# Scores and transposed keys from one series of products, in a gated linear attention with a feed-forward net

## The chip, the cores and the metric

The kernel runs on one core of a Trainium2 chip. The metric is the device time of one execution in microseconds. Three runs of the kernel before gave 528.78 to 529.15 us, median 529.03 us. Its profiled execution took 527.96 us, with a span of 526.4 us from the first to the last instruction.

## The reference

Two parts follow each other. The first is a gated linear attention over 4 batches of 8 heads, 768 tokens and 48 channels a head, with a 48 x 48 state for each head; the second is a feed-forward net on the 3072 x 384 result, with 2048 hidden channels and an exact gelu.

```python
for t in range(S):
    state = alpha[:, :, t, :, None] * state + np.einsum('bhd,bhe->bhde', k[:, :, t], v[:, :, t])
    y[:, :, t] = np.einsum('bhd,bhde->bhe', q[:, :, t], state)
...
h = x @ w_in
g = 0.5 * h * (1.0 + erf(h * inv_sqrt2))
return (g @ w_out).astype(np.float32)
```

## The kernel before

**Units.** The tokens are worked in 12 groups g of 256 (three groups make a batch) and two halves u of four heads: 24 units, numbered n = 2g + u. Names carry both, as s_6_0 for g = 6, u = 0. For each unit, alpha, keys and queries lie in one tile `akq0` or `akq1` (by g), with channels on partitions: two heads of 48 channels in the two halves of 64 partitions, two such pairs, and 256 tokens in four chunks of 64.

**The steps of a unit.** VectorE scans alpha forward (L256) and multiplies the queries by the running products, in place (L261; from the fourth group on GpSimd does this). It scans backward (L265) and multiplies the keys (L268). TensorE then forms the scores of each chunk (`scores`, L284: 16 products with 64 columns of keys as weights and 64 columns of queries moving, each in a quadrant of the array) and transposes the keys (`turned`, L293: four 128 x 128 transposes), both into one two-bank PSUM tile `s`. ScalarE copies the transposed keys out (`turned_out`, tile kn, L300), VectorE masks the scores (`masked`, tile ss, L305). TensorE's step `inside` takes 16 products of masked scores with values (L326) and 16, or 12 in the last group of a batch, of transposed keys with values (the keys' products, L344), into the PSUM tile `ybank`. VectorE adds the latter up to states (`chain`, L361 and L363), and TensorE's `outer` adds states times queries (L390). ScalarE and VectorE split the result into a high and a low part x (L438, L442; in the first groups with a product by -1, the step minus, L447, that leaves the rest in PSUM), and small DMAs complete the tile.

**The net.** A step (g, f) takes 256 tokens and 256 of the 2048 hidden channels: gemm1 (L469, 18 products), the gelu twice on ScalarE (L481 rounded, L482 full), the low part as their difference (L487 on VectorE, or by L491 and L495), and gemm2 (L508, 12 products) into two accumulators. When the steps pass to another group, the accumulators are copied or added to a tile `part` (L525 on ScalarE, L523 and L527 on VectorE). The weights come as 64-bit floats in 16 pieces, a to p, converted by VectorE (L187, L193, L206, L215, L224, L234) and ScalarE (L183, L203) into a high and a low tile (wih and wil, woh and wol).

**The order of work.** All steps are objects with an engine, a cost from the table `COST`, dependencies and a rank; the string `ORDER` ranks the units (numbers) and the pieces (letters). A planner in the kernel simulates the engines with these costs, picks the ready step of least rank, and gives the engines their instructions in that order. `late` units yield to the net's steps; `RATE` and others model the DMAs. So a changed cost moves steps on all engines.

```python
ORDER = "0 1 a b 2 c 3 d 4 e 5 f g h i j k l m n o p"
...
d["scores"] = op("PE", "scores", lambda: (scores(g, u), turned(g, u)), [d["back"], d["q"], p.get("mask"), p.get("kn")], rank=r)
d["kn"] = op("ACT", "kn", lambda: turned_out(g, u), [d["scores"], p.get("inside")], rank=-1)
d["mask"] = op("DVE", "mask", lambda: masked(g, u), [d["scores"], p.get("inside")], rank=-1)
```

Of the kernel before, what the change touches and what calls it, by code (L numbers as in the profile page):

```python
# [8 lines left out]
F32 = mybir.dt.float32  # L9
# [6 lines left out]
ALU = mybir.AluOpType  # L16
# [24 lines left out]
def gla_then_gelu_ffn(ctx: ExitStack, tc: tile.TileContext, q, k, v, alpha, akq, w_in, w_out, out):  # L41
    nc = tc.nc
# [60 lines left out]
    for i in range(NB):  # L103
        vbuf.append(const.tile([P, 2, H * D + DR], F32, name=f"vn{i}"))
        data.append(const.tile([P, NU, 3, 2, G], F32, name=f"akq{i}"))

    for t in vbuf:
# [139 lines left out]
    def ahead(g, u):  # L247
# [3 lines left out]
        pe = work.tile([P, 2], F32, tag="pe", bufs=6, name=f"pe_{g}_{u}")  # L251
        cur[g, u] = dict(pe=pe, qt=qt, kt=kt)

# [18 lines left out]
    def ends_batch(g, j):  # L272
        return g % GPB == GPB - 1 and j == NCH - 1

    def scores(g, u):
        d = cur[g, u]
        d["s"] = ps_s.tile([P, 2, BANK], F32, tag="s", name=f"s_{g}_{u}")
        for i in range(2):
            for j in range(NCH):
                c, o = j // 2, slice((j % 2) * CS, (j % 2 + 1) * CS)  # L280
                t, e = slice(j * CS, (j + 1) * CS), (2 * i + c) * CS
# [6 lines left out]
    def turned(g, u):  # L288
        d = cur[g, u]
        for i in range(2):  # L290
            for c in range(2):
                e = (2 + c) * C
                nc.tensor.transpose(  # L293
                    out=d["s"][:, i, e : e + C], in_=d["kt"][:, i, c * C : (c + 1) * C], identity=ident
                )

    def turned_out(g, u):
        d = cur[g, u]
        d["kn"] = work.tile([P, 2, 2 * P], F32, tag="kn", bufs=1, name=f"kn_{g}_{u}")
        nc.scalar.copy(d["kn"], d["s"][:, :, 2 * C : 4 * C])  # L300

    def masked(g, u):
        d = cur[g, u]
        d["ss"] = work.tile([P, 2, NCH, CS], F32, tag="ss", bufs=1, name=f"ss_{g}_{u}")
        nc.vector.tensor_tensor(  # L305
            out=d["ss"],
            in0=d["s"][:, :, : 2 * C].rearrange("p h (c t) -> p h c t", t=CS),
            in1=mask.unsqueeze(1).unsqueeze(1).to_broadcast([P, 2, NCH, CS]),
            op=ALU.mult,
        )  # L310
# [4 lines left out]
    def inside(g, u):  # L315
        d = cur[g, u]
        vn = vbuf[g % NB]
        for i in range(2):
            for j in range(NCH):
                c, b = j // 2, j % 2  # L320
                r, t = slice(b * CS, (b + 1) * CS), (2 * i + c) * CS
                for h in range(2):
# [10 lines left out]
                    )  # L333
        for j in range(NCH):
            if ends_batch(g, j):
                continue
            c, b = j // 2, j % 2
            r = slice(b * CS, (b + 1) * CS)
            for i in range(2):
                t = 2 * C + (2 * i + c) * D  # L340
                for h in range(2):
                    o = slice(h * DP, (h + 1) * DP)
                    e = (4 * u + 2 * i + h) * D
                    nc.tensor.matmul(  # L344
                        ybank[o, b, t : t + D],
                        lhsT=d["kn"][r, i, c * P + h * DP : c * P + (h + 1) * DP],
                        rhs=vn[r, c, e : e + D],
                        start=False,
                        stop=True,
                        skip_group_check=True,  # L350
                    )

# [24 lines left out]
    def outside_part(g, u):  # L377
        d = cur[g, u]
        for c in range(NCH // 2):
            for i in range(2):  # L380
                for bb, h in ((0, 0), (0, 1), (1, 0), (1, 1)):
                    b = bb if g >= NSB else bb ^ h
                    j = 2 * c + b
                    if g % GPB == 0 and j == 0:
# [7 lines left out]
                        lhsT=states[u][j][r, i],  # L392
                        rhs=d["qt"][r, i, j * CS : (j + 1) * CS],
                        start=False,
# [261 lines left out]
    def plan_unit(n):  # L656
# [171 lines left out]

    bus, lanes, used_lanes = [0.0], [0.0] * LANES, [0]

# [142 lines left out]
```

## Time and profile before

| | |
|---|---|
| median of three runs | 529.03 us |
| profiled execution | 527.96 us |
| its span | 526.4 us |
| mean granted TensorE clock | 0.977 |
| TensorE (PE) busy | 504.8 us, 96% |
| VectorE (DVE) busy | 303.9 us, 58% |
| ScalarE (ACT) busy | 221.4 us, 42% |
| GpSimd (POOL) busy | 33.1 us, 6% |

The granted clock is a share of full speed: 1.00 is 2.4 GHz, 0.50 is 1.2 GHz. PEld is TensorE's weight load, which runs beside the products. A row of the time line gives the start, the duration, the engine, the line, what it writes and reads, how many instructions are drawn together, and in brackets how long the engine was idle before it and what it then waited for. A row of the chain gives start, duration and what ran, on the path that ended last; a product of 32-bit floats leaves two records, so 16 products are x32 there.

### The profile page before, as it was taken

Reading aid. Unit: us, or ns where it says so; the run is one execution under the profiler, and the core shown is the slowest. Engines: PE = TensorE matmul, PEld = TensorE weight load, DVE = VectorE, ACT = ScalarE, POOL = GpSimd, SP = SyncE. Lnnn points to the kernel's source line nnn. Section 1 sums busy time; section 2 is a strip of 40 time slices with the busy share of each in tenths; the row PEclk is TensorE's granted clock in tenths of the full one; section 3 lists DMA queues with packets and bytes.
Section 4 is the critical chain, followed back from the end, with each engine's and each line's share of the span. In section 5 each row is a group of like instructions: output and inputs, shape, how many; then the busy total and the mean of one; then the engine's idle time right before and its main releaser. Section 6 shows DMA issues by size and latency. Waiting matters only on the chain.

```text
span 526.4 us, 13851 instructions
## 1 busy us (share of the span) xinstructions
PE 504.8 (96%) x5994; PEld 487.1 (93%) x5994; DVE 303.9 (58%) x599; ACT 221.4 (42%) x462; POOL 33.1 (6%) x45
## 2 busy tenths in 40 slices
PE   6689899989999999999999999999999999999996
PEld 6578889989999999999999999999999999999995
DVE  6999999999948675866765677142242121211211
ACT  2466767545444454543545345343423222222221
POOL 1000010000001100100100010000000000000000
PEclk9559999999999999999999999999999999999999
DMA  8866472243012423422323322000000000000001
GB/s 307 322 197 212 136 227 88 94 121 121 1 60 79 152 76 92 129 80 68 121 77 97 128 65 78 1 32 17 1 32 16 1 30 1 32 0 1 31 1 34
DMA packets 15249, 44.20 MB, mean 84 GB/s; under 512 B 2224, under 2 KB 5728, under 8 KB 15184
## 3 DMA queue, kind: packets, MB, share of 16 engines
q1 hardware_dynamic: 13520, 38.44, 22.3%
q0 software_dynamic: 1232, 4.33, 2.3%
q8 instruction: 49, 0.80, 0.6%
q10 hardware_dynamic: 432, 0.49, 0.3%
q14 instruction: 16, 0.13, 0.1%
HBM read 36.18 MB, written 4.72 MB: 78 GB/s over the span
## 4 chain that ended last, share of the span: by engine, by line
PE 80%; DVE 13%; DMA 3%; issue 2%; ACT 1%; SPq 0%; DVEq 0%; ACTq 0%
PE hp L469 35%; PE acc L508 35%; PE ybank L390 2%; DVE rp L265 2%; PE ybank L326 2%; PE s L293 2%; PE s L284 2%; DVE pp L256 2%; PE ybank L344 2%; DMA st<-in_moe_w_in_dram 1%; DVE w L193 1%; DMA akq<-in_akq_dram 1%; DVE st L224 1%; DVE u L187 1%; DVE state L363 1%
## 5 line engine op out<-in xcount | busy, mean ns | idle before, releaser
L469 PE MATMUL hp<-x,wih 128*128 128x256 f32 x1152 | 213.7, 286 | 0.0
L469 PEld LDWEIGHTS hp<-x,wih 128*128 128x128 f32 x1152 | 183.2, 192 | 0.8
L469 PE MATMUL hp<-x,wil 128*128 128x256 f32 x576 | 163.5, 284 | 0.0
L481 ACT ACTIVATE ghi<-hp 128x512 fp32r<-128x512 f32 x96 | 57.5, 599 | 226.1 <-PE hp L469 224.2
L487 DVE TENSOR_TENSOR glo<-hp,ghi 128x512 fp32r<-128x512 f32 x86 | 59.3, 690 | 155.7 <-ACT hp L482 155.7
L508 PE MATMUL acc<-woh,ghi 128*128 128x384 f32 x384 | 131.8, 343 | 2.2 <-ACT part L525 1.5
L508 PE MATMUL acc<-wol,ghi 128*128 128x384 f32 x384 | 128.7, 335 | 0.0
L469 PEld LDWEIGHTS hp<-x,wil 128*128 128x128 f32 x576 | 110.7, 192 | 0.0
L508 PE MATMUL acc<-woh,glo 128*128 128x384 f32 x384 | 82.3, 335 | 0.4 <-DVE glo L487 0.4
L508 PEld LDWEIGHTS acc<-woh,ghi 128*128 128x128 f32 x384 | 72.3, 188 | 3.7 <-ACT part L525 1.7
L508 PEld LDWEIGHTS acc<-wol,ghi 128*128 128x128 f32 x384 | 72.5, 189 | 0.1
L508 PEld LDWEIGHTS acc<-woh,glo 128*128 128x128 f32 x384 | 67.9, 188 | 0.7 <-DVE glo L487 0.7
L482 ACT ACTIVATE hp<-hp 128x512 f32<-128x512 f32 x96 | 57.1, 594 | 0.0
L265 DVE TENSOR_TENSOR_SCAN rp<-akq,rp,top 128x255 f32<-128x255 f32 x48 | 39.0, 852 | 0.2
L261 POOL TENSOR_TENSOR akq<-akq,pp 128x512 f32<-128x512 f32 x18 | 23.3, 1293 | 232.9 <-DVE pe L257 183.8
L256 DVE TENSOR_TENSOR_SCAN pp<-akq,top 128x256 f32<-128x256 f32 x48 | 30.4, 675 | 9.4 <-DMA akq<-in_akq_dram 9.4
L390 PEld LDWEIGHTS ybank<-akq,state 48*48 48x48 f32 x704 | 15.6, 125 | 9.1 <-DVE state L363 5.1
L363 DVE TENSOR_TENSOR state<-ybank,state 128x96 f32<-128x96 f32 x80 | 20.5, 256 | 6.1 <-PE ybank L344 3.8
L442 DVE TENSOR_TENSOR x<-ybank,x 64x256 fp32r<-64x256 f32 (+3 forms) x54 | 19.2, 356 | 7.2 <-ACT x L438 6.3
L390 PE MATMUL ybank<-akq,state 48*48 48x64 f32 x704 | 19.3, 228 | 4.2 <-DVE state L363 4.2
L438 ACT CAST x<-ybank 64x256 fp32r<-64x256 f32 (+4 forms) x60 | 19.9, 332 | 7.1 <-PE ybank L390 6.4
L326 PEld LDWEIGHTS ybank<-ss,vn 64*64 64x64 f32 x768 | 14.2, 141 | 9.1 <-DVE ss L305 2.8
(67 smaller groups left out, 410.2 us busy)
## 6 DMA issues: line engine op xcount, KB each, us to landing
akq<-in_akq_dram SPq DMA_DIRECT2D x22, 768.0 KB, 4.8
st<-in_moe_w_in_dram SPq DMA_DIRECT2D x8, 768.0 KB, 4.5
st<-in_moe_w_out_dram SPq DMA_DIRECT2D x8, 768.0 KB, 4.5
vn<-in_v_dram SPq DMA_DIRECT2D x12, 384.0 KB, 3.6
out_dram<-part POOLq DMA_DIRECT2D x11, 384.0 KB, 3.4
x<-z SPq DMA_DIRECT2D x63, 32.0 KB, 2.0
akq<-in_akq_dram SPq DMA_DIRECT2D x2, 512.0 KB, 4.9
akq<-in_akq_dram SPq DMA_DIRECT2D x2, 256.0 KB, 3.4
```

What stands on the lines that cost most here:

```text
L256: nc.vector.tensor_tensor_scan(pp[:, i], at[:, i], top, MID, ALU.mult, ALU.min)
L261: (nc.vector if g < NSB else nc.gpsimd).tensor_tensor(out=qt, in0=qt, in1=pp, op=ALU.mult)
L265: nc.vector.tensor_tensor_scan(rp[:, i, G - 2 :: -1], at[:, i, G - 1 : 0 : -1], top[:, 1:], rp[:, i, G - 1 :], ALU.mult, ALU.min)
L326: nc.tensor.matmul(ybank[o, b, t : t + CS], lhsT=vn[r, c, e : e + DP], rhs=d["ss"][r, h, 2 * i + c, :], start=(i == 0 and c == 0), stop=(j ...
L363: d["chain"] = nc.vector.tensor_tensor(out=st[j + 1], in0=new, in1=st[j], op=ALU.add)
L390: ins = nc.tensor.matmul(ybank[o, b, t : t + CS], lhsT=states[u][j][r, i], rhs=d["qt"][r, i, j * CS : (j + 1) * CS], start=False, stop=Tru ...
L438: nc.scalar.copy(hi, y)
L469: nc.tensor.matmul(hp[:, j, :], lhsT=a[:, j, i * P : (i + 1) * P], rhs=x[:, i, :], start=(j == 0 and i == 0 and n == 0), stop=(i == NK - 1 ...
L481: nc.scalar.activation(ghi, hp, AF.Gelu)
L482: nc.scalar.activation(hp, hp, AF.Gelu)
L487: nc.vector.tensor_tensor(out=glo, in0=hp, in1=ghi.bitcast(F32), op=ALU.subtract)
L508: nc.tensor.matmul(acc[t], lhsT=a[:, j, t * C : (t + 1) * C], rhs=w[:, j, :], start=(first and j == 0 and k == 0 and w is wo_hi[f]), stop= ...
```

## The change

A tile qk0 or qk1 (by u) holds the queries times the running products, and behind each chunk's 64 columns 48 columns of an identity matrix, written once at the start by GpSimd. The scores' 16 products move these 112 columns, so that each gives a chunk's scores and its transposed keys; the four transposes are gone. ScalarE's copy is 384 columns wide, into one fixed tile. The keys' products run in another order, in which the two row halves b alternate. The multiplication of the queries writes to qk, for which it waits for outer of the unit before the last; the load of the next keys no longer waits for outer. The planner has lower costs for scores, kn and inside, a lower DMA rate with a later beginning, and another `ORDER`. GpSimd's DMA ring is smaller.

```diff
@@ planner's table
-RATE, ALONE, LATENCY, SMALL = 400e3, 290e3, 2.1, 50e3
+RATE, ALONE, LATENCY, SMALL, BEGIN = 350e3, 290e3, 2.1, 50e3, 2.2
-    scan=1.62, back=2.05, q=1.35, qv=0.62, scores=1.2, kn=0.6, mask=0.62, inside=1.2, chain=1.15, outer=0.85, carry=0.26,
+    scan=1.62, back=2.05, q=1.35, qv=0.62, scores=1.0, kn=0.5, mask=0.62, inside=1.05, chain=1.15, outer=0.85, carry=0.26,
-ORDER = "0 1 a b 2 c 3 d 4 e 5 f g h i j k l m n o p"
+ORDER = "0 a 1 2 b c 3 d 4 e 5 6 f 7 g h i j k l m n o p"
@@ constants
+    KW = CS + D
+    qk = [const.tile([P, 2, NCH, KW], F32, name=f"qk{i}") for i in range(NU)]
+    for t in qk:
+        for h in range(2):
+            r = slice(h * DP, (h + 1) * DP)
+            eye = ident[r, h * DP : h * DP + D].unsqueeze(1).unsqueeze(1)
+            nc.gpsimd.tensor_copy(t[r, :, :, CS:], eye.to_broadcast([DP, 2, NCH, D]))
@@ ahead, queries
-            (nc.vector if g < NSB else nc.gpsimd).tensor_tensor(out=qt, in0=qt, in1=pp, op=ALU.mult)
+            eng = nc.vector if g < NSB else nc.gpsimd
+            eng.tensor_tensor(out=qs[:, :, :, :CS], in0=by_chunk(qt), in1=by_chunk(pp), op=ALU.mult)
@@ scores
-                        d["s"][o, h, e : e + CS], lhsT=d["kt"][r, i, t], rhs=d["qt"][r, i, t], start=True, stop=True
+                        d["s"][o, h, e : e + KW], lhsT=d["kt"][r, i, t], rhs=d["qs"][r, i, j], start=True, stop=True
@@ turned
-                nc.tensor.transpose(
-                    out=d["s"][:, i, e : e + C], in_=d["kt"][:, i, c * C : (c + 1) * C], identity=ident
-                )
@@ turned_out
-        nc.scalar.copy(d["kn"], d["s"][:, :, 2 * C : 4 * C])
+        nc.scalar.copy(to, blocks(g, u)[..., CS:])
@@ inside, the keys' products
-        for j in range(NCH):
...
-            c, b = j // 2, j % 2
-            r = slice(b * CS, (b + 1) * CS)
+        for c in range(NCH // 2):
             for i in range(2):
...
+                for b in range(2):
+                    if ends_batch(g, 2 * c + b):
+                        continue
+                    r = slice(b * CS, (b + 1) * CS)
+                    for h in range(2):
...
+                            lhsT=kn[r, at : at + DP],
@@ plan_unit
-        used = [old.get(k) for k in ("outer", "scores", "c0", "c1")]
+        used = [old.get(k) for k in ("q", "scores", "c0", "c1")]
-        d["q"] = op(e, cost, lambda: fns["q"](), [d["scan"], d["rest"]], rank=r)
+        d["q"] = op(e, cost, lambda: fns["q"](), [d["scan"], d["rest"], pp_.get("outer")], rank=r)
-        d["scores"] = op("PE", "scores", lambda: (scores(g, u), turned(g, u)), [d["back"], d["q"], p.get("mask"), p.get("kn")], rank=r)
+        d["scores"] = op("PE", "scores", lambda: scores(g, u), [d["back"], d["q"], p.get("mask"), p.get("kn")], rank=r)
@@ the program
-    nc = _bacc.Bacc("TRN2", target_bir_lowering=False, num_devices=1)
+    nc = _bacc.Bacc("TRN2", target_bir_lowering=False, num_devices=1, dynamic_dma_scratch_size=8192)
```

What moves on the engines is shown at three places, where an x behind a row counts equal instructions in a row.

TensorE in the steady part, about the steps (3, 4) and (3, 5) of the net, before: the end of gemm2, the later half of outer, and scores and transposes of unit 12 behind it.

```order
L390 MATMUL ybank_137<-akq1_120,state0_2_125 48x64 x2
L390 MATMUL ybank_137<-akq1_120,state0_3_126 48x64 x2
L390 MATMUL ybank_137<-akq1_120,state0_2_125 48x64 x2
L390 MATMUL ybank_137<-akq1_120,state0_3_126 48x64 x2
L284 MATMUL s_6_0_2659<-akq0_118 64x64 x16
L293 MATMUL s_6_0_2659<-ident_76,akq0_118 128x128 x4
L469 MATMUL hp_3_5_2685<-x3_1919,wih5_143 128x256 x2
```

The same stretch in the change, the end of outer and what follows it:

```order
L399 MATMUL ybank_145<-qk0_121,state0_3_134 48x64 x2
L399 MATMUL ybank_145<-qk0_121,state0_2_133 48x64 x2
L399 MATMUL ybank_145<-qk0_121,state0_3_134 48x64 x2
L478 MATMUL hp_3_5_2583<-x3_1874,wih5_151 128x256 x2
L478 MATMUL hp_3_5_2583<-x3_1874,wil5_159 128x256
```

and, one gemm1 and one gemm2 later, the scores of unit 12:

```order
L517 MATMUL acc0_3_0_2329<-woh4_166,glo_3_4_2607 128x384 x2
L517 MATMUL acc1_3_0_2330<-woh4_166,glo_3_4_2607 128x384 x2
L299 MATMUL s_6_0_2634<-qk0_121,akq0_118 64x112 x16
L517 MATMUL acc0_3_0_2329<-woh5_167,ghi_3_5_2628 128x384
L517 MATMUL acc0_3_0_2329<-wol5_175,ghi_3_5_2628 128x384
```

Scores that stood right behind outer now stand between two gemm2.

ScalarE about the first finished accumulators (tile part2), before:

```order
L183 ACTIVATE u_10_1490<-st_10_1288 128x768
L481 ACTIVATE ghi_0_3_1506<-hp_0_3_1460 128x512
L482 ACTIVATE hp_0_3_1460<-hp_0_3_1460 128x512
L203 CAST wih5_143<-w_10_1509 128x768
L525 COPY part2_175<-acc0_2_0_1316 128x384
L525 COPY part2_175<-acc1_2_0_1317 128x384
L481 ACTIVATE ghi_0_4_1553<-hp_0_4_1515 128x512
```

and in the change:

```order
L490 ACTIVATE ghi_0_3_1457<-hp_0_3_1419 128x512
L491 ACTIVATE hp_0_3_1419<-hp_0_3_1419 128x512
L193 ACTIVATE u_10_1462<-st_10_1344 128x768
L534 COPY part2_183<-acc0_2_0_1298 128x384
L534 COPY part2_183<-acc1_2_0_1299 128x384
L213 CAST wih5_151<-w_10_1488 128x768
L490 ACTIVATE ghi_0_4_1508<-hp_0_4_1466 128x512
```

The copies of the accumulators now stand ahead of the cast of wih5 and no longer behind it.

VectorE at the start, from the query multiplication of unit 1 on, before:

```order
L261 TENSOR_TENSOR akq0_118<-akq0_118,pp_0_1_203 128x512
L265 SCALAR_TENSOR_TENSOR rp_0_1_204<-akq0_118,rp_0_1_204,top_114 128x255 x2
L268 TENSOR_TENSOR akq0_118<-akq0_118,rp_0_1_204 128x512
L305 TENSOR_TENSOR ss_0_0_239<-s_0_0_210,mask_133 128x512
L187 TENSOR_SCALAR u_0_231<-u_0_231 128x768
L193 SCALAR_TENSOR_TENSOR w_0_276<-st_0_183,u_0_231 128x768
```

and in the change:

```order
L276 TENSOR_TENSOR qk1_122<-akq0_118,pp_0_1_211 128x8x64
L313 TENSOR_TENSOR ss_0_0_237<-s_0_0_218,mask_141 128x512
L280 SCALAR_TENSOR_TENSOR rp_0_1_212<-akq0_118,rp_0_1_212,top_114 128x255 x2
L283 TENSOR_TENSOR akq0_118<-akq0_118,rp_0_1_212 128x512
L197 TENSOR_SCALAR u_0_239<-u_0_239 128x768
L370 COPY state0_1_132<-ybank_145 128x96
```

The mask of unit 0 has moved ahead of unit 1's backward scan.

## Rows read from the trace of the kernel before

**Rows 1.** The page's part 1: busy us, share of the span, instructions.

```profile
PE 504.8 (96%) x5994; PEld 487.1 (93%) x5994; DVE 303.9 (58%) x599; ACT 221.4 (42%) x462; POOL 33.1 (6%) x45
```

**Rows 2.** Windows, us: stretch and length, engines' busy time, granted clock, DMA share, GB/s.

```profile
7.20:14.10 6.90, 4.26 (x102) 3.76 (x104) 6.34 (x13) 2.82 (x6) 0.00 (x0) 1.00 1.03 401
14.10:38.00 23.90, 17.58 (x303) 15.44 (x298) 23.21 (x48) 12.72 (x24) 0.00 (x0) 0.50 0.77 269
38.00:57.20 19.20, 16.60 (x342) 14.41 (x340) 18.27 (x35) 12.43 (x25) 0.00 (x0) 1.00 0.51 162
57.20:110.00 52.80, 50.69 (x614) 48.00 (x613) 50.56 (x88) 33.95 (x67) 6.45 (x5) 1.00 0.43 145
110.00:510.00 400.00, 398.87 (x4556) 389.09 (x4555) 199.50 (x410) 155.55 (x337) 25.08 (x24) 1.00 0.18 55
```

**Rows 3.** Chain of waits, 169.5 to 188 us: start, duration, what ran.

```profile
173.10 0.62 PE s L284 x32
173.72 0.59 PE s L293 x4
...
176.47 2.09 PE acc L508 x12
178.56 0.62 PE ybank L326 x32
179.18 0.50 PE ybank L344 x30
179.68 2.30 PE acc L508 x12
...
184.13 0.59 PE ybank L390 x32
184.72 0.47 PE s L284 x32
185.19 0.59 PE s L293 x4
185.78 2.16 PE hp L469 x18
```

**Rows 4.** Chain of waits, 62 to 72.5 us, a unit with twelve keys' products.

```profile
66.33 0.44 PE ybank L344 x22
```

**Rows 5.** Time line, 9.5 to 13 us, the first unit's way.

```profile
9.53 0.70 PE L284 MATMUL s<-akq 48*64 48x64 f32 x32
...
10.15 1.39 DVE L265 TENSOR_TENSOR_SCAN rp<-akq,rp,top 128x255 f32<-128x255 f32 x2
...
11.98 0.57 ACT L300 COPY kn<-s 128x512 f32<-128x512 f32 x1
...
12.66 0.69 DVE L305 TENSOR_TENSOR ss<-s,mask 128x512 f32<-128x512 f32 x1 [0.39 <-ACT kn L300]
```

**Rows 6.** Time line, the first gemm1 and the outer behind it; unit 4's outer.

```profile
34.25 0.79 PE L469 MATMUL hp<-x,wih 128*128 128x256 f32 x2
...
38.24 1.10 PE L390 MATMUL ybank<-akq,state 48*48 48x64 f32 x32
...
56.12 1.10 PE L390 MATMUL ybank<-akq,state 48*48 48x64 f32 x32 [1.35 <-DVE state L363]
```

**Rows 7.** Time line, three waits of TensorE behind 57 us.

```profile
77.13 0.50 PE L491 MATMUL hp<-ghi,minus 128*128 128x512 f32 x1 [0.65 <-ACT hp L482]
...
108.38 0.83 ACT L203 CAST wih<-w 128x768 fp32r<-128x768 f32 x1 [2.24 <-DVE w L193]
...
109.12 0.85 ACT L525 COPY part<-acc 128x384 f32<-128x384 f32 x2
...
109.64 0.44 PE L508 MATMUL acc<-woh,ghi 128*128 128x384 f32 x1 [1.46 <-ACT part L525]
...
118.41 1.01 DVE L523 TENSOR_TENSOR part<-part,acc 128x384 f32<-128x384 f32 x2
...
119.10 0.41 PE L508 MATMUL acc<-woh,ghi 128*128 128x384 f32 x1 [0.73 <-ACT ghi L481]
```

More of the change, by code (lines that the diff above doesn't have):

```diff
@@ L105, in gla_then_gelu_ffn @@
         data.append(const.tile([P, NU, 3, 2, G], F32, name=f"akq{i}"))
+    KW = CS + D
[5 more added lines that the diff above has]
+            nc.gpsimd.tensor_copy(t[r, :, :, CS:], eye.to_broadcast([DP, 2, NCH, D]))
+    kn = const.tile([P, 2 * NCH * D + DR], F32, name="kn")
+    nc.gpsimd.memset(kn[:, 2 * NCH * D :], 0.0)
     for t in vbuf:
@@ L251, in ahead, with by_chunk @@
         pe = work.tile([P, 2], F32, tag="pe", bufs=6, name=f"pe_{g}_{u}")
-        cur[g, u] = dict(pe=pe, qt=qt, kt=kt)
+        qs = qk[u]
+        cur[g, u] = dict(pe=pe, qs=qs, kt=kt)
+        def by_chunk(x):
+            return x.rearrange("p i (j t) -> p i j t", t=CS)
         def forward():
@@ L280, in scores @@
                 c, o = j // 2, slice((j % 2) * CS, (j % 2 + 1) * CS)
-                t, e = slice(j * CS, (j + 1) * CS), (2 * i + c) * CS
+                t, e = slice(j * CS, (j + 1) * CS), (2 * i + c) * KW
                 for h in range(2):
@@ L284, in scores, with blocks @@
                     nc.tensor.matmul(
-                        d["s"][o, h, e : e + CS], lhsT=d["kt"][r, i, t], rhs=d["qt"][r, i, t], start=True, stop=True
+                        d["s"][o, h, e : e + KW], lhsT=d["kt"][r, i, t], rhs=d["qs"][r, i, j], start=True, stop=True
                     )
[L288 to L292, printed above, removed]
-                nc.tensor.transpose(
-                    out=d["s"][:, i, e : e + C], in_=d["kt"][:, i, c * C : (c + 1) * C], identity=ident
-                )
+    def blocks(g, u):
+        return cur[g, u]["s"][:, :, : NCH * KW].rearrange("p h (c t) -> p h c t", t=KW)
     def turned_out(g, u):
-        d = cur[g, u]
-        d["kn"] = work.tile([P, 2, 2 * P], F32, tag="kn", bufs=1, name=f"kn_{g}_{u}")
-        nc.scalar.copy(d["kn"], d["s"][:, :, 2 * C : 4 * C])
+        to = kn[:, : 2 * NCH * D].rearrange("p (h c d) -> p h c d", h=2, d=D)
+        nc.scalar.copy(to, blocks(g, u)[..., CS:])
     def masked(g, u):
@@ L306, in masked @@
             out=d["ss"],
-            in0=d["s"][:, :, : 2 * C].rearrange("p h (c t) -> p h c t", t=CS),
+            in0=blocks(g, u)[..., :CS],
             in1=mask.unsqueeze(1).unsqueeze(1).to_broadcast([P, 2, NCH, CS]),
@@ L333, in inside @@
                     )
-        for j in range(NCH):
-            if ends_batch(g, j):
-                continue
-            c, b = j // 2, j % 2
-            r = slice(b * CS, (b + 1) * CS)
+        for c in range(NCH // 2):
             for i in range(2):
                 t = 2 * C + (2 * i + c) * D
[L341 to L351, printed above, removed]
+                for b in range(2):
[3 more added lines that the diff above has]
+                    for h in range(2):
+                        o = slice(h * DP, (h + 1) * DP)
+                        e = (4 * u + 2 * i + h) * D
+                        at = (h * NCH + 2 * i + c) * D
+                        nc.tensor.matmul(
+                            ybank[o, b, t : t + D],
+                            lhsT=kn[r, at : at + DP],
+                            rhs=vn[r, c, e : e + D],
+                            start=False,
+                            stop=True,
+                            skip_group_check=True,
+                        )
     def chain(g, u):
@@ L392, in outside_part @@
                         lhsT=states[u][j][r, i],
-                        rhs=d["qt"][r, i, j * CS : (j + 1) * CS],
+                        rhs=d["qs"][r, i, j, :CS],
                         start=False,
@@ L827, in gemm1_op @@
         return st["gemm1"]
-    bus, lanes, used_lanes = [0.0], [0.0] * LANES, [0]
+    bus, lanes, used_lanes = [BEGIN], [0.0] * LANES, [0]
     def place(o, t):
```

## Prediction

> **What bounds the kernel now.** I read the page's busy times first, then busy times by stretch, then the chain of waits and the time line in the places the change touches. TensorE is busy for 96% of the span [rows 1], but that is a mean over stages. The stretches [rows 2] show the stages: from 14.1 to 57.2 us VectorE is nearly full (23.21 of 23.90 us, then 18.27 of 19.20) while TensorE has 6.3 and 2.6 us idle, and until 38 us TensorE is granted 0.50, the lower of its two levels (1.2 GHz), after a stretch in which it was idle for 2.6 of 6.9 us. From 57.2 us on TensorE is the bound: 2.1 us idle up to 110 us, 1.1 us in the 400 us after. So a microsecond of TensorE work is worth a microsecond behind 57 us and close to nothing ahead of it; ahead of it VectorE's order counts. Nineteen of the 24 units (a unit is 256 tokens of four heads) run their TensorE steps behind 57 us.
>
> **One unit on TensorE.** The chain in order of time around 170 to 186 us [rows 3] shows two units' steps between the big products. Scores alone after gemm2 take 0.62 us, the four transposes 0.59: a run of 1.21. When the scores follow outer, they take 0.47, so 0.15 is the price of entering the quadrant products. A gemm2 behind inside takes 2.30, against 2.09 behind gemm1: 0.21 is the price of leaving them. Outer alone costs 0.59 + 0.21 = 0.80, scores with transposes alone 1.21, and the two joined 0.59 + 0.47 + 0.59 = 1.65: a join saves 0.36.
>
> **Scores with identity columns.** The 16 products move 112 columns instead of 64, with the same 64 columns of weights. Upper bound: in proportion, 0.47 x 112/64 = 0.82. Lower bound: 0.47, if the weights set the pace; the keys' products, with 48 moving columns, speak for it, since sixteen of them take 0.50, no less than sixteen scores [rows 3]. Against it stands outer, whose weights have 48 columns instead of 64 and which still takes 0.59 against the 0.62 of lone scores: a quarter less weights, 5% less time. So I stay near the upper bound and take 0.78, a little under it for what each product has fixed. A lone run then costs 0.15 + 0.78 + 0.21 = 1.14, against 1.21; joined to outer 0.59 + 0.78 + 0.21 = 1.58 against 1.65. That is -0.07 a unit, **-1.3 us** over 19 (at 0.82: -0.6; at 0.47: -7.2).
>
> **Joins lost.** The planner has new costs, and the order of TensorE's steps moves. In before, 14 of these 19 units have their scores behind outer or behind inside, and in the change 6; the first piece of order in the section on the change shows one such pair come apart. Eight joins at 0.36 are **+2.9 us** (if entering and leaving overlap with the neighbours where no join is, half of it: +1.4).
>
> **Row halves.** In before sixteen keys' products take 0.50 us [rows 3] and twelve 0.44 [rows 4]: four more cost only 0.06, so the two row halves already run beside each other, and what alternation can remove is the end where only one half is left. Twelve of the 19 units have sixteen products: 12 x 0.06 = **-0.7 us** (ends: 0 and the -2.6 of the first rival).
>
> **Stalls.** Three stalls of TensorE behind 57 us have a cause that the order takes away [rows 7]. At 77.13 it waits 0.65 us on ScalarE's second gelu: gone, other steps now stand between. At 109.64 it waits 1.46 on the copy of the finished accumulators (109.12), which on ScalarE's queue stood behind the cast of a weight piece (108.38), itself waiting 2.24 for VectorE; now the copies stand ahead of that cast (second piece of order). At 119.10 it waits 0.73; the row names the gelu, but VectorE's add into the part started at 118.41, late behind a conversion, and now stands ahead of it. Together -2.84. A new one comes: scores, minus and inside of unit 6 stand in a row, so inside waits for the kn copy and the mask. These take 0.57 and 0.69 in the first unit [rows 5] and run one behind the other, some 1.4 us with their hand-overs, covered by 0.45 us of minus: +0.95. Net **-1.9 us** (from -2.8, if the new wait finds cover, to -0.9, if the copy at 109 is still late by 1.0 because the piece before it comes later).
>
> **The early part.** The third piece of order shows VectorE: the first unit's mask moves ahead of the second unit's backward scan. Today it stands behind it and waits 0.39 us, at 12.66 [rows 5]. In its new place VectorE comes to it at about 10.2, where that scan now starts, while scores that start at 9.53 and take 0.9 us, and kn's 0.57, end near 11.1: a wait of some 0.9 us, so 0.5 us more than now. A second such mask, unit 2's, stands nearer to its scores too: 0.5 more. The identity copies, four on GpSimd, run beside VectorE's first scans and may slow them by up to a microsecond, of which the 0.9 us wait takes most. So VectorE is 1 to 2 us late by 45 us. Against that, outer of unit 4, for which TensorE now waits 1.35 us with nothing in between [rows 6], has a gemm1 ahead of it in the new order, which fills the wait. I take **0** (-1.5 if the lag is absorbed, +1.5 if it is twice as long).
>
> **At nothing**: ScalarE's copy of 384 instead of 512 columns (its wait is off TensorE's path once steps stand between); the two instructions a unit that scatter queries to a new tile (same elements; they now wait for outer of the unit before last, which is long done, and the load of the next keys no longer does); the smaller ring for GpSimd's stores, which are 20 us and more apart; the planner's lower DMA rate, which only moves the issue of loads.
>
> **Sum**: -1.3 + 2.9 - 0.7 - 1.9 + 0 = -1.0, on the profiled execution's 527.96 us. That execution lies 1.07 us under the median of the three runs, 529.03; the difference is taken to be the same for the median: **528.0 us**.
>
> **Rivals.**
> (1) The keys' products gain in full from alternating. If the four in one row half hold each other up, then apart they go at the pace of their 48 columns: 0.47 x 48/64 = 0.35 for sixteen (-0.15) and 0.33 for twelve (-0.11): 12 x 0.15 + 7 x 0.11 = 2.6, which is 1.9 more than in the sum: 526.1. For it: before issues four in a row of one half. Against: 0.50 for sixteen is already the pace of scores, which alternate. The Trainium skill ("TensorE: Matmul & The Clock Gate", Part 3, The mechanism) says that a weight load overlaps products in flight only when its row group differs, which is the rule by which this rival would come true; the equal pace in the chain does not bear it out. Chance 0.17.
> (2) The early part gains: the mask's wait is shorter than I think, while the filled wait at 56 us and earlier FFN steps count: -1.5 on top, 526.5. For it: TensorE has 8.9 us idle before 57 us [rows 2]. Against: VectorE is full there. Chance 0.13. With it goes the case that the weights set the pace of the scores, 3 us and more faster, chance 0.03.
> (3) Slower: the lag of VectorE reaches TensorE with its clock. The place is unit 4's outer, at 56 us in before. The lag decides if it is over the 1.35 us that the gemm1 fills; and if TensorE is thin between 39 and 50 us, it may be granted 0.50 again, as it was from 14.1 us on after a thin stretch. One gemm1 at that level takes from 34.25 to 38.24 us [rows 6], at the full one 2.16 [rows 3], so +1.8; the lag in excess gives +0.5 to +1.5. With 2.7 us more than the sum: 530.7. For it: every early wait that I can work out in the new order is longer. Against: VectorE's work has not grown. Chance 0.17.
> (4) The change does not do what it says for TensorE: the products of 112 columns cost the full proportion, entries and exits as much as joins lost, and new waits take the place of the three stalls: +0.7 on the scores and +0.9 on stalls, 529.6. Chance 0.10.
>
> **Numbers.** The forecast has 0.40, with a range of its own from 526.9 to 529.1. A measurement of this kernel can tell some 0.2%, 1.06 us, from no change, so faster means under 527.97 and slower over 530.09. Half of the forecast, 0.20, lies on either side of the first bound; (1) and (2) are faster (0.33); (3) gives 0.13 slower and 0.04 same; (4) 0.08 same and 0.02 slower. Faster 0.53, same 0.32, slower 0.15. The range goes from 525.0, which takes in (1) and (2) with an early gain or a stall more, to 530.6, just short of (3)'s full price: about 0.2 is left out, at its two ends.
>
> **What would show it.** Scores near 0.78 us joined and 0.94 alone in the chain; keys' products near 0.47 for sixteen; a gemm2 or gemm1 0.2 longer behind lone scores; no waits at 77, 109 and 119 us, and one of about 1 us ahead of unit 6's inside; VectorE's first mask waiting near 0.9 us; the start of the steady part within 1.5 us of now. The prediction is wrong in its main term if scores take 0.6 us or less, or if keys' products fall to 0.35; wrong in its early term if the clock's rise comes at another time than 38 us or the granted clock falls behind it.

## The result and the profile after

The changed kernel takes 522.78 us in the median of five runs (522.47 to 523.9), the kernel before 529.03 (528.65 to 529.48). The ratio is 0.9889, with a 95% interval from 0.9868 to 0.991: 6.2 us faster. The forecast was 528.0, with a range from 525.0 to 530.6, so the time lies below the range. The direction was right, the size was not.

The profiled execution took 522.47 us, 5.49 us less than that of before. Its page, busy us, share and instructions of each engine, against [rows 1]:

```profile
PE 501.1 (96%) x5898; PEld 480.8 (92%) x5898; DVE 299.3 (57%) x599; ACT 219.1 (42%) x462; POOL 35.5 (7%) x50
```

Busy times by stretch, columns and stretches as in [rows 2] (the last ends at 505):

```profile
7.20:14.10 6.90, 4.34 (x139) 3.86 (x140) 6.61 (x15) 2.94 (x6) 0.00 (x0) 1.00 1.04 401
14.10:38.00 23.90, 17.84 (x291) 15.75 (x283) 22.88 (x46) 14.51 (x28) 0.00 (x0) 0.64 0.74 272
38.00:57.20 19.20, 15.71 (x275) 14.09 (x277) 18.65 (x37) 10.92 (x25) 0.00 (x0) 0.82 0.51 168
57.20:110.00 52.80, 51.95 (x633) 49.36 (x630) 49.17 (x84) 34.43 (x66) 3.90 (x3) 1.00 0.47 158
110.00:505.00 395.00, 395.00 (x4475) 381.86 (x4474) 196.39 (x411) 152.37 (x335) 27.61 (x26) 1.00 0.17 54
```

VectorE still fills the stretches up to 57 us. TensorE's idle time falls from 2.1 to 0.85 us between 57 and 110 us, and to nothing behind it. The lower clock comes in two pieces now, one of them behind 38 us; together they last 23.9 us, as the one piece did before.

The chain in the steady part, to be held against [rows 3]:

```profile
160.56 0.62 PE ybank L334 x32
161.18 0.45 PE ybank L353 x32
161.63 2.31 PE acc L517 x12
163.94 0.59 PE ybank L399 x32
164.54 2.32 PE hp L478 x18
166.85 2.12 PE acc L517 x12
168.97 0.93 PE s L299 x32
169.90 2.32 PE hp L478 x18
```

Scores of 112 columns stand alone (0.93 us), outer stands alone (0.59), and each is followed by a gemm of 2.3 us: the exits are paid (the price of leaving the quadrant products, 2.32 against 2.15 for a gemm1). The keys' products take 0.45 us, not 0.50. And the chain near the end, where groups 10 and 11 of the net follow each other with nothing between:

```profile
472.08 2.15 PE hp L478 x18
474.23 2.08 PE acc L517 x12
476.31 2.15 PE hp L478 x18
478.46 2.08 PE acc L517 x12
480.55 2.04 PE hp L478 x18
482.59 2.09 PE acc L517 x12
484.67 2.04 PE hp L478 x18
```

From 480.55 us on gemm1 takes 2.04 us instead of 2.15. Nothing in the diff touches gemm1. This is the first step of group 11. Counted per product, from the start of a step's second product to that of its last, groups 3, 7 and 11 run at 113.3 ns in 16 of their 24 steps (113.2 to 113.4), at 114.3 in two and at 117.6 to 117.8 in six; all others run at 119.1 to 120.1 once the clock is up, as all twelve groups do in the kernel before (118.7 to 120.1).

Where the time went, by the start of the same step in both traces (the order of these steps is the same in both):

| from, to | before | after | difference |
|---|---|---|---|
| start to scores of unit 5 | 62.11 | 60.85 | -1.3 |
| to gemm2 of step (1, 4) | 61.31 | 58.26 | -3.0 |
| to gemm1 of step (0, 6) | 19.02 | 19.02 | 0.0 |
| to gemm1 of step (8, 0), the steps of 16 units | 238.94 | 238.57 | -0.4 |
| to gemm1 of step (11, 7) | 133.32 | 132.57 | -0.7 |

### The profile page after: what moved, and what is told of

It is laid out like the page before. It is cut to its first block, busy times and chain, and to the rows that moved or that the text cites. A ratio compares the mean times of both kernels' runs of the same rounds, so it can differ in the third digit from the quotient of the medians.

```text
span 520.9 us, 13668 instructions
## 1 busy us (share of the span) xinstructions
PE 501.1 (96%) x5898; PEld 480.8 (92%) x5898; DVE 299.3 (57%) x599; ACT 219.1 (42%) x462; POOL 35.5 (7%) x50
## 4 chain that ended last, share of the span: by engine, by line
PE 85%; DVE 9%; ACT 2%; DMA 1%; issue 1%; ACTq 0%; DVEq 0%
PE hp L478 38%; PE acc L517 37%; PE s L299 3%; PE ybank L399 3%; PE ybank L334 2%; PE ybank L353 2%; DVE pp L270 1%; DVE rp L280 1%; DVE st L234 1%; DVE w L203 1%; DMA st<-in_moe_w_in_dram 1%; DVE wil L244 1%; DVE u L225 1%; DMA akq<-in_akq_dram 1%; DVE u L216 1%
## 5 line engine op out<-in xcount | busy, mean ns | idle before, releaser
L276 POOL TENSOR_TENSOR qk<-akq,pp 128x512 f32<-128x512 f32 x18 | 23.3, 1294 | 206.7 <-PE ybank L399 85.6
L280 DVE TENSOR_TENSOR_SCAN rp<-akq,rp,top 128x255 f32<-128x255 f32 x48 | 34.1, 752 | 0.2
L308 ACT COPY kn<-s 128x384 f32<-128x384 f32 x24 | 11.5, 481 | 43.6 <-PE ybank L353 29.3
L299 PE MATMUL s<-qk,akq 48*64 48x112 f32 x768 | 25.7, 274 | 3.6 <-DVE akq L283 3.5
L299 PEld LDWEIGHTS s<-qk,akq 48*64 48x64 f32 x768 | 20.4, 140 | 7.2 <-issue 5.8
L542 POOL DMA_DIRECT2D out_dram<-part x11 | 8.3, 753 | 243.0 <-DVE part L536 154.1
```

The costliest lines, as they stand in the source:

```text
L276: eng.tensor_tensor(out=qs[:, :, :, :CS], in0=by_chunk(qt), in1=by_chunk(pp), op=ALU.mult)
L280: nc.vector.tensor_tensor_scan(rp[:, i, G - 2 :: -1], at[:, i, G - 1 : 0 : -1], top[:, 1:], rp[:, i, G - 1 :], ALU.mult, ALU.min)
L299: nc.tensor.matmul(d["s"][o, h, e : e + KW], lhsT=d["kt"][r, i, t], rhs=d["qs"][r, i, j], start=True, stop=True)
```

## The experiments

**Is it the place of the tile?** In the program's layout, the addresses in a partition of gemm1's weights leave a remainder of 224 when divided by 256 in the kernel before, and so do those of all x tiles. In the changed kernel the new constant tiles and the work tile kn that is gone shift everything that is allocated behind them: weights and the x ring now leave 32, but the tile of groups 3, 7 and 11, allocated from the other end, still leaves 224. So it lies 192 bytes off the weights, by 256. The first run moves it back.

```diff
-            x = late[0].tile([P, NK, 2, G], F32R, tag="xl", name=f"x{g}")
+            x = late[0].tile([P, NK * 2 * G + 48], F32R, tag="xl", name=f"x{g}")
+            x = x[:, : NK * 2 * G].rearrange("p (k i t) -> p k i t", k=NK, i=2)
```

> The changed kernel, with the tile of x of the groups 3, 7 and 11 moved down by 192 bytes in each partition, so that its address leaves the same remainder by 256 as those of the weights (32; in the changed kernel it leaves 224). In the changed kernel gemm1 of these groups shows 113.3 ns a product in 19 of its 24 steps and 117.6 in the other five, all other groups 119.3; in the kernel before all twelve groups show 119.3. Theory A, the remainder decides: groups 3, 7 and 11 go back to 119.3 ns, and the time rises by 24 steps x 18 products x some 5 ns = 1.9 to 2.3 us over the changed kernel's 522.8, to about 524.8. Rival B, something else in the change (its order, the smaller copy, the fixed tile) makes these groups fast: they stay at 113.3 ns and the time at 522.8.

(Its 19 and five steps are a rougher count of the 16, two and six above.) Measured: 525.59 us, ratio to before 0.9932 [0.991, 0.9955], against the changed kernel's 0.9889 [0.9868, 0.991]. The chain in group 11:

```profile
486.97 2.15 PE hp L479 x18
489.12 2.08 PE acc L518 x12
491.20 2.15 PE hp L479 x18
```

gemm1 is back at 2.15, in groups 3 and 7 too. Between the step marks of the table above it takes 239.64 and 133.32 us, 1.07 and 0.75 more than the changed kernel: 1.8 us of the change's gain is this address. Another 1.2 us between the two profiles lies ahead of unit 5, which starts at 62.01; that part differs from run to run, as the early part below shows. So the medians, which differ by 2.8 us, would put too much down to the address.

**Which distances count?** The next run gives each tile of the ring its own distance.

```diff
-            x = ffn.tile([P, NK, 2, G], F32R, tag="x", bufs=XB, name=f"x{g}")
+            x = ffn.tile([P, NK * 2 * G + 16], F32R, tag="x", bufs=XB, name=f"x{g}")
...
-        ghi = ffn.tile([P, 2, G], F32R, tag="ghi", name=f"ghi_{g}_{f}")
+        ghi = ffn.tile([P, 2 * G + 16], F32R, tag="ghi", name=f"ghi_{g}_{f}")[:, : 2 * G].rearrange("p (j t) -> p j t", j=2)
```

> The changed kernel, with each x tile of the ring of three longer by 64 bytes, and each tile of the high and low parts of gelu too. So x of groups 0, 4, 8 lies 0 bytes from the remainder of the weights by 256, of groups 2, 6, 10 64 bytes, of groups 1, 5, 9 128 bytes, and of groups 3, 7, 11 192 bytes as in the changed kernel; the high part's two tiles lie 192 and 0, the low part's 64 and 128 from the weights of gemm2. Theory A: gemm1 stays at 119.3 ns a product in groups 0, 4, 8 and falls to about 113 in those of the other groups whose distance counts; six groups at 113.3 would be 48 steps x 18 x 6 ns = 5.2 us less, 517.6. For gemm2 (173.6 ns a product throughout) the same theory expects less where high or low part lies apart from its weights, some 6 ns too. Rival B: only the tile at the upper end of the memory is fast, the others stay at 119.3, and the time at 522.8.

Measured: 524.01 us, 0.991 [0.9882, 0.9938]. A later run did the same at odd multiples of 32:

> The changed kernel with every tile that gemm1 and gemm2 move placed at another odd multiple of 32 bytes from its weights, by 256: x of groups 0, 4, 8 at 32, of groups 2, 6, 10 at 96, of 1, 5, 9 at 160, of 3, 7, 11 at 224; the two tiles of gelu's high part at 32 and 96, of its low part at 160 and 224. Theory A, the pace of a product goes with the distance by 256 as in the sweep by 64 bytes (119.3 at 0, 117.8 at 64, 118.4 at 128, 113.3 to 117.8 at 192): each group's pace lies between those of its neighbours, 113 to 119, and gemm2 stays between 172 and 178. Rival B, the rule is only whether two addresses are equal by 64: all groups fall to 113.3 or less, and gemm2 too.

It took 525.07 us in its only execution (before: 528.15). Nanoseconds of one product of gemm1, steps of groups 3 to 11, both runs together:

| distance by 256 | 0 | 32 | 64 | 96 | 128 | 160 | 192 | 224 |
|---|---|---|---|---|---|---|---|---|
| ns | 118.7 to 120.1 | 116.6 to 116.9 | 117.8, 117.9 | 119.6 to 120.2 | 118.2 to 119.9 | 117.2 to 118.9 | 113.3, 114.7, 117.8 | 117.9 to 118.5 |

So the pace goes with the distance by 256, and not with whether the addresses are equal by 64; 192 is the best by far. It is not the place of the x tile by itself: x that leaves 224 is fast in the changed kernel, whose weights leave 32, and slow in the kernel before, whose weights leave 224. gemm2 showed 173.2 to 177.1 ns a product at the distances of these two runs (medians 174.6 and 175.3), and 173.3 to 176.0 (median 173.6) in late_in_phase, where all lie at 0: no gain there, and by an estimate from these medians 1 to 2 us lost over the 96 steps. That may be one reason why neither sweep beats the changed kernel. At 192 there is more than one pace: in the first sweep's group 11 it changes from step to step between 114.7 and 117.8, as the two buffers of each gelu tile take turns. What sets that was not found.

**The whole of it, in both kernels.** All x tiles at the distance 192, the gelu tiles left at 0: in the changed kernel, and in the kernel before with nothing of the change (there the tile of groups 3, 7 and 11 moves too, by 64 bytes down).

```diff
+    ffn.tile([P, 48], F32, tag="pad", bufs=1, name="pad")
...
-        cur[g, "z"] = ffn.tile([P, 2, G], F32R, tag="z", bufs=1, name=f"z{g}")
+        cur[g, "z"] = ffn.tile([P, 2 * G + 16], F32R, tag="z", bufs=1, name=f"z{g}")[:, : 2 * G].rearrange("p (i t) -> p i t", i=2)
```

> The changed kernel with all x tiles of the ring moved up by 192 bytes, so that each leaves 224 by 256 where the weights leave 32, as the tile of groups 3, 7 and 11 already does; the tiles of gelu's parts stay at 32, like gemm2's weights. Theory A: gemm1 takes 113.3 to 117.7 ns a product in all twelve groups, 72 steps x 18 x 1.6 to 6.0 ns = 2.1 to 7.8 us less, about 516 to 517 at the shares seen in groups 7 and 11. Rival B: only one place in memory gives the gain: 119.3 ns in the nine groups, 522.8.

> The kernel before, nothing of the change in it, with all x tiles moved so that they leave 160 by 256 where the weights leave 224 (the same distance of 192 as in the fast groups of the changed kernel); the tiles of gelu's parts stay at the weights' remainder. Theory A, the distance of the addresses alone makes gemm1 faster: 96 steps x 18 products x 1.6 to 6 ns, at the shares of the changed kernel with all tiles moved (about nine steps in ten at 113.3 where scores and outer stand apart, fewer where they alternate) 6 to 9 us under before, 520 to 523. Rival B, it needs the changed order or the lack of transposes: no difference, 528 to 529.

Measured: the changed kernel 518.16 us, 0.9807 [0.9785, 0.9828]; the kernel before 519.67, 0.9826 [0.9792, 0.986]. Both beat both kernels of the case, and the kernel before with a pad of 192 bytes beats the change. Its chain:

```profile
474.37 2.04 PE hp L471 x18
476.41 2.09 PE acc L510 x12
478.50 2.04 PE hp L471 x18
```

The changed kernel came out dearer than expected (516 to 517): gemm1 runs at 117.5 to 118.1 ns in 21 of its 96 steps, all of them in groups 0 to 7, which have units' steps between their own. Counted by 1024, the fast distances in these two runs and the changed kernel are 192, 448 and 704, so a period of 256 fits all of them. With the addresses alike in both, the rest of the change is worth 1.5 us by these medians, and 3.4 with all x tiles at 0 (late_in_phase, 525.59 against 528.99 of before beside it); the intervals are too wide to tell which.

**The keys' products.** Only their loop goes back to the old order.

```diff
-        for c in range(NCH // 2):
-            for i in range(2):
...
-                for b in range(2):
+        for j in range(NCH):
...
+            c, b = j // 2, j % 2
+            r = slice(b * CS, (b + 1) * CS)
+            for i in range(2):
```

> The changed kernel with the keys' products in their old order (four of one row half in a row). Its chain shows 0.45 us for sixteen against 0.50 before. Theory: the end where one row half is left comes back, 0.05 us for each of 12 units with sixteen products in the steady part, so +0.6 us at most, 523.4, and 0.50 us in the chain. Rival: alternating takes more off than its own duration shows (a weight load that now overlaps in inside as a whole), 2 us and more: 525.

Measured: 523.77 us, 0.9913 [0.9888, 0.9938]; not to be told from the changed kernel by its time, but its chain shows what was asked:

```profile
161.87 0.62 PE ybank L334 x32
162.49 0.50 PE ybank L353 x30
162.99 2.29 PE acc L517 x12
```

0.50 against 0.45, and 239.07 against 238.57 us from step (0, 6) to (8, 0): 0.5 us for the alternation. The rival that put it at 2.6 us is out. The rule of the Trainium skill ("TensorE: Matmul & The Clock Gate", Part 3, The mechanism) that a weight load overlaps products in flight only when its row group differs would make rows of four of one half dear; the same section also lets a load go ahead into a background weight buffer. Here such rows cost 0.05 us over sixteen products.

**Why the joins were lost.** A third tile for queries and identity.

```diff
-    qk = [const.tile([P, 2, NCH, KW], F32, name=f"qk{i}") for i in range(NU)]
+    qk = [const.tile([P, 2, NCH, KW], F32, name=f"qk{i}") for i in range(NQ)]
...
-        qs = qk[u]
+        qs = qk[(NU * g + u) % NQ]
...
-        d["q"] = op(e, cost, lambda: fns["q"](), [d["scan"], d["rest"], pp_.get("outer")], rank=r)
+        d["q"] = op(e, cost, lambda: fns["q"](), [d["scan"], d["rest"], unit.get(n - 3, {}).get("outer")], rank=r)
```

> The changed kernel with three tiles for queries and identity instead of two, used in turn, so that the multiplication of a unit's queries waits for outer of the unit three before it, not two. With two tiles the scores of unit n+2 cannot follow outer of unit n at once: GpSimd has to multiply queries first (1.29 us) into the tile that outer has just read. The planner then puts scores behind outer in 16 units of the steady part, against 2 in the changed kernel and 13 in the kernel before. Theory A, the shared tile lost the joins, and each is worth 0.36 us: 10 to 14 joins, 3.6 to 5.0 us less than the changed kernel, 517.8 to 519.2, and the chain shows scores at 0.77 behind outer. Rival B, the joins are worth less because lone outer and scores cost no exits of their own: no more than 1 us less. Rival C, the scores move ahead and meet GpSimd's multiplication late, with new waits: 522 or more.

> Both edits together: three query tiles and all x tiles off the weights' remainder. If joins and addresses are independent costs of TensorE, their gains add: 3.6 to 5.0 plus 5 to 7.5 us under 522.8, 510.5 to 514. If not, because other engines bound once TensorE is faster, it stays at 515 or more.

Measured: 527.05 us, 0.9981 [0.996, 1.0001]; with the addresses moved too, 522.85, 0.9884 [0.9847, 0.992]. Both are worse than the same kernel with two tiles; the addresses are worth 4.2 us here, against 4.6 with two tiles. The joins came back: 13 runs of outer and scores between 140 and 390 us take 1.36 us up to the next gemm, where outer and scores apart take 0.59 and 0.93 and one exit more. But TensorE is idle for 4.3 us between 138 and 385 us, in the changed kernel not at all. The order of the net's steps differs too, from step (1, 5) on. Three of the waits, and what VectorE did ahead of the third, from the time line:

```profile
150.20 0.41 PE L517 MATMUL acc<-woh,ghi 128*128 128x384 f32 x1 [1.30 <-DVE part L532]
...
166.68 0.41 PE L517 MATMUL acc<-woh,ghi 128*128 128x384 f32 x1 [0.69 <-DVE part L532]
...
168.80 1.39 DVE L280 TENSOR_TENSOR_SCAN rp<-akq,rp,top 128x255 f32<-128x255 f32 x2
170.23 0.69 DVE L283 TENSOR_TENSOR akq<-akq,rp 128x512 f32<-128x512 f32 x1
170.84 1.13 DVE L372 TENSOR_TENSOR state<-ybank,state 128x96 f32<-128x96 f32 x4
...
172.02 0.66 PE L399 MATMUL ybank<-qk,state 48*48 48x64 f32 x32 [1.93 <-DVE state L372]
```

The add into the states stands behind the backward scan and the multiplication of the keys for the coming scores. Behind the wait at 172 us the granted clock falls to 0.50 for a while: 0.76 in the mean of 172 to 176, and the gemm1 that starts at 173.6 us takes 199 ns a product. Theory A is half right: the shared tile did lose the joins. The time is rival C's, but not its mechanism, since TensorE waits for VectorE's adds and not for GpSimd's multiplication: the waits that the two tiles save are worth more than the joins.

**Planner and products apart.** The old products with the new planner, and the reverse (the whole of the first hunk of the change's diff, applied or taken back); then the changed kernel with the old string, the old DMA model, and the old costs, one line at a time.

```diff
-ORDER = "0 a 1 2 b c 3 d 4 e 5 6 f 7 g h i j k l m n o p"
+ORDER = "0 1 a b 2 c 3 d 4 e 5 f g h i j k l m n o p"
...
-RATE, ALONE, LATENCY, SMALL, BEGIN = 350e3, 290e3, 2.1, 50e3, 2.2
+RATE, ALONE, LATENCY, SMALL, BEGIN = 400e3, 290e3, 2.1, 50e3, 0.0
...
-    scan=1.62, back=2.05, q=1.35, qv=0.62, scores=1.0, kn=0.5, mask=0.62, inside=1.05, chain=1.15, outer=0.85, carry=0.26,
+    scan=1.62, back=2.05, q=1.35, qv=0.62, scores=1.2, kn=0.6, mask=0.62, inside=1.2, chain=1.15, outer=0.85, carry=0.26,
```

> The kernel before with the changed planner alone: its costs, its order of units and pieces, its DMA rate and beginning; scores, transposes, copies and the keys' products as before, and the addresses of the tiles as before. If the planner's new order brings the gain up to 121 us (4.3 us by the steps of the two traces: the wait before unit 4's outer, and the waits at 77, 109 and 119 us), it runs 3 to 4 us under 529.0 less what it loses by fewer joins of scores to outer (8 x 0.36 = 2.9) and with all gemm1 at 119.3 ns: about 527.5 to 529. Rival: the gain up to 121 us comes from the shorter scores and copies, and the order alone, made for shorter costs than it meets, is slower than before: 530 or more.

> The changed kernel with the old planner: costs, order, DMA rate and beginning of the kernel before; scores of 112 columns, no transposes, alternating row halves, and the changed addresses. By the parts: scores 19 x -0.07 = -1.3, keys' products 12 x -0.05 = -0.6, gemm1 of three groups -2.0, so 525.1 from 529.0, with the waits at 56, 77, 109 and 119 us still there and scores mostly joined to outer. Rival: the planner is worth the greater part, and it runs at 527 or more, or the old order finds shorter waits in the early part by itself and runs at 522 to 523.

> The changed kernel with the old string of units and pieces alone; its costs and its DMA model stay. If the string carries the gain of the early part and of the three waits (some 3 us up to 120 us in the mean of the runs with the changed kernel's early part), this runs at 525 to 527 and a wait stands before unit 4's outer or at 109 us. If the costs or the DMA model carry it, it runs at 522 to 524.

> The changed kernel with the old DMA rate and beginning in the planner alone. ScalarE's first weight piece then stands ahead of the first kn copy again, and waits for its load up to 11.2 us as in the kernel before; inside of unit 0, which starts at 11.2 us in the changed kernel, waits to 13.4 or later, and VectorE's mask with it. If this order at the start carries the gain, it is 1.3 to 3 us slower than the changed kernel, 524 to 526; if VectorE's later work takes the slack up, as before 57 us VectorE is full, it stays within 1 us of it.

> The changed kernel with the old costs of scores, kn and inside alone. The planner still puts 12 scores alone and one behind outer in the steady part, so the lost joins do not hang on these costs. If the costs carry the early gain, it is slower by 1 to 3 us, 524 to 526; else within 1 us of the changed kernel.

Measured, with the start of unit 5's scores and of gemm2 of step (0, 3), the one that waited at 109.64 us in the kernel before:

| kernel | us | ratio to before, interval | unit 5 | (0, 3) |
|---|---|---|---|---|
| before | 529.03 | 1 | 62.11 | 109.64 |
| new planner, old products | 530.26 | 1.0026 [1.0007, 1.0044] | 63.56 | 110.73 |
| old planner, new products | 527.46 | 0.9975 [0.9953, 0.9996] | 64.61 | 110.30 |
| old string alone | 525.02 | 0.9932 [0.9909, 0.9955] | 63.05 | 112.81 |
| old DMA model alone | 527.32 | 0.9979 [0.9958, 1.0001] | 64.86 | 110.41 |
| old costs alone | 529.04 | 1.0008 [0.9987, 1.003] | 60.61 | 110.77 |
| changed | 522.78 | 0.9889 [0.9868, 0.991] | 60.85 | 106.41 |

(With the old string, (0, 3) has other steps of the net ahead of it, and with the old costs unit 5 has, so these two entries are to be read with care.) Neither half brings the gain: the products with the old planner gain 1.5 us, which is no more than the address gives, and the new planner with the old products loses 1.3. Taking back any one of the planner's three parts loses 2 to 6 of the 6.2 us. Part of what the halves need of each other stands in the first 15 us. With the new planner and the old products, VectorE's first mask has moved up, but scores with transposes and the wider copy end late:

```profile
11.80 0.69 DVE L305 TENSOR_TENSOR ss<-s,mask 128x512 f32<-128x512 f32 x1 [1.60 <-ACT kn L300]
```

With the new products and the old DMA model, ScalarE's copy stands behind the first weight piece, which waits for its load (all of the 4.0 us that this profile loses on the changed one lie ahead of unit 5):

```profile
11.37 0.89 ACT L193 ACTIVATE u<-st 128x768 f32<-128x768 f32 x1 [9.14 <-DMA st<-in_moe_w_in_dram]
...
12.15 0.47 ACT L308 COPY kn<-s 128x384 f32<-128x384 f32 x1
...
12.72 0.69 DVE L313 TENSOR_TENSOR ss<-s,mask 128x512 f32<-128x512 f32 x1 [2.48 <-ACT kn L308]
```

In the changed kernel neither happens:

```profile
9.82 0.48 ACT L308 COPY kn<-s 128x384 f32<-128x384 f32 x1 [7.60 <-PE s L299]
...
10.40 0.69 DVE L313 TENSOR_TENSOR ss<-s,mask 128x512 f32<-128x512 f32 x1
```

(In the first of these three profiles the clock rose late, at 7.8 us; with the same late rise the new products, in x_off_phase, wait 1.25 us and not 1.60.) Another part stands in the steady part. The old products need no shared tile, and with them the new planner puts scores behind outer in 16 units, where the expectation had fewer joins than before. From step (0, 6) to (8, 0) this run takes 240.77 us, 1.8 more than the kernel before, with TensorE idle for 2.4; the longest wait is the one that the three tiles met too:

```profile
152.96 0.41 PE L508 MATMUL acc<-woh,ghi 128*128 128x384 f32 x1 [1.30 <-DVE part L523]
```

With the old costs, TensorE waits in other places, one of them for the small DMAs that complete x, and behind these waits the clock is granted at 0.50 again, from 55.8 to 59.2 us; gemm1 of step (2, 3) starts 4.7 us later than in the changed kernel:

```profile
54.45 0.50 PE L500 MATMUL hp<-ghi,minus 128*128 128x512 f32 x1 [1.45 <-ACT hp L491]
...
56.07 0.77 PE L478 MATMUL hp<-x,wih 128*128 128x256 f32 x2 [1.12 <-DMA x<-z]
```

## Why the prediction was wrong

- **The missing term.** This is the step that failed outright. gemm1 was taken as unchanged, 2.16 us [rows 3], and the "At nothing" list has no word on where tiles lie. The change adds and removes tiles, and so moved x of three groups against its weights: 1.8 us. This is the one part of the gain that neither products nor planner made.
- **The stalls** were the right mechanism, mis-sized. Forecast: -2.84 and +0.95, net -1.9. Measured: the three waits are gone, and TensorE's idle time between 61 and 121 us falls from 2.84 to 0.85. The new wait ahead of unit 6's inside came, with 0.74 us; the row names ScalarE's copy of the rest of x, which ended at 70.86, but the mask, for which the prediction had it wait, ended at 70.82.

```profile
70.13 0.69 DVE L313 TENSOR_TENSOR ss<-s,mask 128x512 f32<-128x512 f32 x1 [0.92 <-ACT kn L308]
...
70.92 0.70 PE L334 MATMUL ybank<-ss,vn 64*64 64x64 f32 x32 [0.74 <-ACT x L462]
```

A wait of 0.40 us at 274.73 us, which the prediction did not list, is gone too, and a wait costs some 0.16 more than its idle time (gemm2 of step (0, 3) gains 1.62 us on the step ahead of it, for an idle time of 1.46). From unit 5 to step (1, 4) the table has -3.0, of which the idle time is 2.0; the rest is not told apart here.
- **The early part**, forecast 0 with bounds of 1.5, came out at -1.3 in this profile, and part of that is luck. Eight profiles have the changed kernel's early order. In them the granted clock first rises to 1.00 between 4.4 and 7.8 us; the first scores, behind the warm-up, start between 8.50 and 9.86 us in the same order, and the first mask's wait goes from none at the earliest to 1.25 us at the latest. In this profile the clock rose at 5.6 us and the mask does not wait; in that of before it rose at 7.3. So the wait of some 0.9 us that the prediction worked out is there when the clock rises late, as in old_k_order (6.8 us) and x_off_phase (7.8 us):

```profile
11.01 0.69 DVE L313 TENSOR_TENSOR ss<-s,mask 128x512 f32<-128x512 f32 x1 [0.76 <-ACT kn L308]
```

```profile
11.49 0.69 DVE L313 TENSOR_TENSOR ss<-s,mask 128x512 f32<-128x512 f32 x1 [1.25 <-ACT kn L308]
```

Unit 2's mask waits 0.36 us, and the identity copies end at 3.9 us, about when VectorE's first scan starts (3.85). What failed is the lag of 1 to 2 us: the eight start unit 5's scores between 60.85 (this profile) and 62.56 us (median 61.9), none of them more than 0.5 behind before. Two profiles with the early order of before have 62.11 and 63.44 (the padded one), so about -0.9 may be the change's; two are too few to be sure. Also wrong was to put the planner's DMA model at nothing: with the old one alone, unit 5 starts at 64.86 us.
- **The scores**: forecast 0.78 behind outer and 0.93 to 0.94 alone; measured 0.77 (three_qk, 1.36 less 0.59) and 0.93. Right.
- **The joins**: forecast 14 to 6 and +2.9 us; the order is as printed. From step (0, 6) to (8, 0) the change gains only 0.4 us, of which 1.1 is the address and 0.4 the wait at 274.73 us, so the units' steps cost 1.1 us more. This stretch loses nine joins, and has 15 scores and eleven insides with sixteen keys' products; at the prediction's prices that is 9 x 0.36 - 15 x 0.07 - 11 x 0.06 = +1.5. The size held, roughly. The cause did not: the prediction blamed the planner's costs, but with the old costs or the whole old planner the scores stay apart, and the new planner with the old products has 16 joins. It is the wait of the query product for outer, which the prediction listed under "at nothing".
- **The row halves**: forecast 0.7 over 19 units, measured 0.5 over the 16 units of that stretch, eleven of them with sixteen products.
- **The rivals.** (1) is refuted by old_k_order. (2) is the direction that the early part took, with luck in it. (3) did happen in part: behind a wait of 2.44 us for VectorE, at 39.89 us, the clock was granted 0.50 again up to 46.5 us, and it had risen at 32.9 us, not 38. Both were named as signs that the early term is wrong; unit 5 still started earlier than before. (4) is out.

```profile
39.89 1.77 PE L299 MATMUL s<-qk,akq 48*64 48x112 f32 x32 [2.44 <-DVE akq L283]
```

- **The median**: 0.8 us of the miss is that the profiled execution of before lies 1.07 us under its median, that of the changed kernel 0.31 under its own.

In sum, the -5.5 of the profiles are -1.3 up to unit 5, -3.0 up to step (1, 4), most of it stalls, -0.4 for the wait at 274.73 us, -1.8 for the address and +1.1 for the units' steps, alternation in them; forecast were 0, -1.9 for all stalls, nothing for the address, and +0.9.

## What to carry to other kernels

List every tile that a change adds, drops or resizes, and look at what it does to the addresses of the tiles that TensorE reads side by side: 192 bytes of padding were worth more here than the whole change. Planner and products may be worth something only together: here the new products under the old planner gained no more than their address, the new planner with the old products lost 1.3 us, and both together gained 6.2. And a new tile that two units share is a new wait: look for who is queued behind its reader before it goes under "at nothing".

## What the runs showed of the hardware

- A product of gemm1 (128 x 128 weights, 256 columns) takes 113.3 to 120.2 ns by the distance of its two operands' addresses by 256; the kernel before gains 8.8 us from moving x alone. It could not be read from any view of the profile before, as all its groups were equal; it showed only when three groups of twelve differed.
- Two runs of quadrant products that follow each other at once take less than apart (outer and scores 1.36 us together, 0.59 and 0.93 apart), and a gemm behind a run of quadrant products takes 0.16 to 0.21 us longer.
- Eight profiles of the same early order started unit 5's scores up to 1.7 us apart. Their first scores, behind the warm-up, started between 8.50 and 9.86 us, in the order in which the clock was first granted at 1.00 (4.4 to 7.8 us).
